# Tile 2's queries and keys in the slots of late weights, tile 3's unit loads one by one

## The chip, the cores and the metric

The kernel runs on one core of a Trainium2 chip. The metric is the device time of one execution in microseconds (us); lower is better. Five engines work side by side, each through its own queue in order: TensorE (PE; its weight loads are PEld), VectorE (DVE), ScalarE (ACT), GpSimd (POOL) and SyncE (SP), which here issues most of the DMA transfers.

## The reference, cut to what matters

Sliding-window attention (4 batches, 8 heads, 576 positions, 64 features, each query sees itself and the 63 positions ahead of it), then two feed-forward layers over the 2304 tokens.

```python
def _attn_ref(q, k, v):
    scores = scale * np.matmul(q, k.transpose(0, 1, 3, 2))
    scores = np.where(mask, scores, -1e9)              # window of 64
    attn = exp(scores - max); attn = attn / (sum + 1e-9)
    return np.matmul(attn, v)

def _moe_ref(x, w_in, w_out):                          # 512 -> 2048 -> 512
    h = x @ w_in
    g = np.where(h >= 1, h, np.where(h <= -1, 0.0, (h + 1) ** 2 / 4))
    return g @ w_out

def _moe2_ref(x, w_in, w_out, g_ln):                   # 512 -> 1024 -> 512
    h = x @ w_in
    solu = h * softmax(h)
    return ((solu - mean) / sqrt(var + 1e-6) * g_ln) @ w_out
```

## The kernel before

Products of 32-bit numbers are made of three products each: every operand is split into a high part (`xh`, `gh`, `wih`, `woh`) and the remainder (`xl`, `gl`, `wil`, `wol`).

The first part of the program does attention and the first feed-forward layer at once. Tokens go in blocks of 384 (`j`), each of two tiles of 192 tokens (`t`); a tile has four groups of two heads (`g = 4 t + hp`). The 2048 features go in 16 ranges of 128 (`f`). For each block and range TensorE makes h (`ps_h`, `moe_h`), ScalarE and VectorE make the activation (`u` by `moe_g2` on VectorE, which is the last to read `ps_h` and so frees its bank; `gh` on ScalarE; `gl`, in block 0 on GpSimd), and TensorE adds it, times w_out, to four sums (`acc`, `moe_y`). `ps_h` has two banks, so a range waits for `u` of the range two before it. In block 0 ranges 0 and 1 go in two halves of 192 tokens. Between the ranges a slot of the attention of the next block is done (`slots`): scores (`ps_s`, `st_s`; VectorE's score reads make `p` and `mx`), probabilities, `ps_x`, and of that `xh` and `xl`.

Block 0 also brings in the weights. They come in 32 units, w_in and w_out of a range in turn (`w1_unit`, loads on SP of 512 KB into the staging tiles `wst`, of which there are five). A unit is prescaled on ScalarE (`split_a`), passed over twice on VectorE (`split_b`, L136 and L137), copied on ScalarE into `wih` or `woh`, and subtracted on VectorE (`split_c`, L146) into `wil` or `wol`. That last pass frees the staging tile for the unit five later. The result stays in SBUF, one slot for each range.

Queries and keys come in two ways (`load_qk`). Groups 0 to 11 (tiles 0 to 2) come a whole tile at a time as rows (`qkn`) and are transposed by TensorE (`st_qkt`, `ps_t`). From group 12 (tile 3) on they come as units, one for each group: eight loads of 24 or 32 KB in pieces of 32 numbers, which VectorE transposes in blocks of 32 x 32 (L331, L332). The rows of tiles 0 and 1 lie in slots of w_in ranges 12 to 15, not yet used; the rows of tile 2 take four of the five tiles `qk`, in which the units lie too. The four units of tile 3 are asked for together, at group 11 (`qkt_and_loads`).

A scheduler sets the order of each engine's queue from its own estimate of times; the code gives dependencies and buffers, and `tc.issue_after(x)` asks that what is traced in it stand behind instruction `x` on the engine of `x`. `wdma` lists the weight loads.

## Time and profile before

| | us |
|---|---|
| median of 3 runs | 706.5 (705.88 to 707.57) |
| the profiled execution | 706.22 |
| its span, first to last instruction | 704.1 |
| TensorE busy in the span | 682.2 |
| VectorE busy | 441.7 |
| ScalarE busy | 412.3 |
| GpSimd busy | 153.8 |

The 2.1 us between the profiled execution's time and its span lie around the first and the last instruction. Busy times are averages over stages with different limits; the rows further down go by stretches of time.

### The profile page before, as it was taken

Reading aid. Unit: us, or ns where it says so; the run is one execution under the profiler, and the core shown is the slowest. Engines: PE = TensorE matmul, PEld = TensorE weight load, DVE = VectorE, ACT = ScalarE, POOL = GpSimd, SP = SyncE. Lnnn points to the kernel's source line nnn. Section 1 sums busy time; section 2 is a strip of 40 time slices with the busy share of each in tenths; the row PEclk is TensorE's granted clock in tenths of the full one; section 3 lists DMA queues with packets and bytes.
Section 4 is the critical chain, followed back from the end, with each engine's and each line's share of the span. In section 5 each row is a group of like instructions: output and inputs, shape, how many; then the busy total and the mean of one; then the engine's idle time right before and its main releaser. Section 6 shows DMA issues by size and latency. Waiting matters only on the chain.

```text
span 704.1 us, 12633 instructions
## 1 busy us (share of the span) xinstructions
PE 682.2 (97%) x4439; PEld 629.4 (89%) x4439; DVE 441.7 (63%) x1179; ACT 412.3 (59%) x1006; POOL 153.8 (22%) x193
## 2 busy tenths in 40 slices
PE   6969999999999999999999999999999999999998
PEld 5858899999999999999999999999987788888887
DVE  4699888356455555454455553642379999988850
ACT  5898877465556655565566565354454746345451
POOL 3432422200001000021112111652272322220000
PEclk9988999999999999999999999999999999999999
DMA  9997486534354524345352211562024465534321
GB/s 188 225 260 227 125 243 152 115 75 108 72 115 107 120 64 78 74 129 130 79 113 70 99 49 42 173 202 90 1 100 124 151 194 168 185 126 142 128 90 46
DMA packets 150391, 87.62 MB, mean 124 GB/s; under 512 B 113464, under 2 KB 136248, under 8 KB 150328
## 3 DMA queue, kind: packets, MB, share of 16 engines
q1 hardware_dynamic: 138888, 62.69, 35.9%
q0 software_dynamic: 8704, 19.41, 8.4%
q10 hardware_dynamic: 2736, 4.72, 1.8%
q8 instruction: 35, 0.57, 0.4%
q14 instruction: 28, 0.23, 0.1%
HBM read 62.66 MB, written 24.12 MB: 123 GB/s over the span
## 4 chain that ended last, share of the span: by engine, by line
PE 78%; DVE 7%; issue 5%; ACT 4%; DMA 2%; POOL 2%; SPq 1%; DVEq 0%; POOLq 0%; ACTq 0%
PE acc L533 25%; PE ps_h L502 24%; PE ps_o L832 13%; PE P L717 8%; PE ps_x L482 2%; PE ps_s L448 2%; PE ps_p L408 2%; POOL wil L249 2%; PE ps_s L358 1%; PE ps_x L427 1%; DVE gl L522 1%; DVE wst L137 1%; DMA wst<-in_moe_w_in_dram 1%; ACT p L372 1%; DMA wst<-in_moe_w_out_dram 1%
## 5 line engine op out<-in xcount | busy, mean ns | idle before, releaser
L517 DVE SCALAR_TENSOR_TENSOR u<-u,ps_h 128x384 f32<-128x384 f32 (+1 forms) x98 | 53.3, 544 | 144.1 <-ACT u L512 143.5
L502 PE MATMUL ps_h<-xh,wih 128*128 128x384 f32 (+1 forms) x392 | 132.4, 339 | 4.6 <-DVE u L517 3.6
L502 PE MATMUL ps_h<-xl,wih 128*128 128x384 f32 (+1 forms) x392 | 132.3, 338 | 1.7 <-DVE xl L435 1.7
L533 PE MATMUL acc<-gl,woh 128*128 128x384 f32 (+1 forms) x392 | 130.7, 334 | 1.6 <-DVE gl L522 1.3
L502 PE MATMUL ps_h<-xh,wil 128*128 128x384 f32 (+1 forms) x392 | 131.9, 337 | 0.0
L533 PE MATMUL acc<-gh,wol 128*128 128x384 f32 (+1 forms) x392 | 129.6, 332 | 0.0
L533 PE MATMUL acc<-gh,woh 128*128 128x384 f32 (+1 forms) x392 | 128.9, 341 | 0.4 <-ACT gh L518 0.4
L511 ACT ACTIVATE u<-ps_h,half 128x384 f32<-128x384 f32 (+1 forms) x98 | 56.1, 573 | 92.3 <-PE ps_h L502 92.1
L518 ACT CAST gh<-u 128x384 fp32r<-128x384 f32 (+1 forms) x98 | 49.7, 507 | 56.1 <-DVE u L517 38.7
L502 PEld LDWEIGHTS ps_h<-xh,wih 128*128 128x128 f32 x392 | 74.5, 191 | 5.9 <-DVE u L517 4.0
L502 PEld LDWEIGHTS ps_h<-xl,wih 128*128 128x128 f32 x392 | 74.7, 191 | 2.7 <-DVE xl L435 2.1
L533 PEld LDWEIGHTS acc<-gl,woh 128*128 128x128 f32 x392 | 73.7, 188 | 2.5 <-DVE gl L522 1.7
L533 PEld LDWEIGHTS acc<-gh,woh 128*128 128x128 f32 x392 | 72.7, 188 | 3.6 <-issue 2.6
L502 PEld LDWEIGHTS ps_h<-xh,wil 128*128 128x128 f32 x392 | 74.8, 191 | 0.2 <-DVE wil L146 0.2
L522 DVE TENSOR_TENSOR gl<-u,gh 128x384 fp32r<-128x384 f32 x80 | 51.0, 638 | 37.4 <-ACT gh L518 36.8
L533 PEld LDWEIGHTS acc<-gh,wol 128*128 128x128 f32 x392 | 73.6, 188 | 0.0
L717 PE MATMUL P<-wih,x2p 128*128 128x512 f32 x216 | 70.8, 391 | 1.4 <-DVE xo L545 0.9
L832 PE MATMUL ps_o<-woh,wol 128*128 128x512 f32 (+1 forms) x152 | 57.7, 380 | 0.3 <-DVE wol L820 0.3
L832 PE MATMUL ps_o<-woh,woh 128*128 128x512 f32 (+1 forms) x152 | 57.7, 379 | 0.0
L832 PE MATMUL ps_o<-wol,woh 128*128 128x512 f32 (+1 forms) x152 | 57.5, 378 | 0.0
L512 ACT ACTIVATE u<-u 128x384 f32<-128x384 f32 (+1 forms) x98 | 51.1, 521 | 2.0
L717 PEld LDWEIGHTS P<-wih,x2p 128*128 128x128 f32 x216 | 40.5, 188 | 10.4 <-DVE xo L545 1.3
(126 smaller groups left out, 1217.0 us busy)
## 6 DMA issues: line engine op xcount, KB each, us to landing
wst<-in_moe_w_in_dram SPq DMA_DIRECT2D x16, 512.0 KB, 5.5
wst<-in_moe_w_out_dram SPq DMA_DIRECT2D x16, 512.0 KB, 5.3
lnd<-e SPq DMA_DIRECT2D x16, 512.0 KB, 2.8
lT<-lnd SPq DMA_DIRECT2D x64, 128.0 KB, 3.0
vw<-in_v_dram SPq DMA_DIRECT2D x24, 256.0 KB, 4.9
x2d<-xo POOLq DMA_DIRECT2D x24, 192.0 KB, 2.4
out_dram<-o ACTq DMA_DIRECT2D x17, 256.0 KB, 2.4
wst<-in_moe_w_in_dram POOLq DMA_DIRECT2D x8, 512.0 KB, 5.5
```

What stands on the lines that cost most here:

```text
L249: nc.gpsimd.tensor_tensor(lo, v_, as_f32(hi), op=ALU.subtract)
L408: nc.tensor.transpose(ps[:, i * 128:i * 128 + 128], p[:, i, :], ident)
L448: nc.tensor.matmul(ps[x][64 * c:64 * c + 64, i * 128 + c0:i * 128 + 128], z[r, KQ + i * 64:KQ + i * 64 + 64], z[r, i * 64 + c0:i * 64 + 12 ...
L502: nc.tensor.matmul(ps, a, bb[:, kc, c], start=(n == 0), stop=(n == 3 * KC - 1))
L511: nc.scalar.activation(u, ps, ACTF.Relu, bias=half, scale=0.5)
L512: nc.scalar.activation(u, u, ACTF.Square)
L517: g = nc.vector.scalar_tensor_tensor(u, u, 1.0, ps, op0=ALU.min, op1=ALU.max)
L518: return nc.scalar.copy(hi, u).ins, g.ins
L522: eng.tensor_tensor(lo, u, as_f32(hi), op=ALU.subtract)
L533: nc.tensor.matmul(acc[j, e][:, c], a, bb, start=(f == 0 and n == 0 and c.start == 0), stop=(f == NF - 1 and n == 2),)
L717: nc.tensor.matmul(ps, l, r, start=(n == 0), stop=(n == 5))
L832: nc.tensor.matmul(ps, a[kk // 4][:, kk % 4, :], b[kk][:, c:c + w], start=(n == 0), stop=(n == 3 * NK2 - 1),)
```

## The change

The rows of tile 2 no longer lie in tiles `qk`: its queries go to the slots `woh14` and `woh15`, its keys to `wol14` and `wol15`, the slots of w_out of the last two ranges. The tiles `qk` are then free for units from the start. The units of tile 3 are asked for one at each of the groups 8 to 11 instead of all at group 11, and each stands behind the weight load issued last (`wdma[-1]`) instead of behind the first one (`wdma[0]`).

```diff
                 for r in range(2):
-                    if t < 2:
-                        a = w_p.tile([128, 512], F32, tag=f"{tag}{14 - 2 * t + r}", name="qkn")
-                    else:
-                        a = at_p.tile([128, 512], F32, tag="qk", bufs=5, name="qkn")
+                    if t == 2:
+                        tag = "woh" if src is q else "wol"
+                    a = w_p.tile([128, 512], F32, tag=f"{tag}{14 - 2 * (t % 2) + r}", name="qkn")
                     dst[t, r] = a[0:n, :]
...
         if m >= NPE and m + 4 < NG:
             load_qk(m + 4)
-        if m == NPE - 1:
-            for z in range(1, 5):
-                after(load_qk, m + z)
+        if NPE - 4 <= m < NPE:
+            with tc.issue_after(wdma[-1]):
+                load_qk(m + 4)
```

The scheduler makes other queues of it. Lines behind the change count one less than before. On VectorE, about the second half of ranges 0 and 1, `wst_626` before and `wst_635` in the change are unit 11, `wil5` is the third pass of unit 10, and `u_729`, `u_812` before are `u_747`, `u_830` in the change. Before, from `xl` on:

```order
L435 TENSOR_TENSOR xl_312<-ps_x_664,xh_311 128x192
L383 TENSOR_SCALAR sm_654<-sm_654 128x3
L136 TENSOR_SCALAR wst_626<-wst_626 128x512
L137 SCALAR_TENSOR_TENSOR wst_534<-wst_534 128x512
L384 RECIPROCAL rs_673<-sm_654 128x3
L137 SCALAR_TENSOR_TENSOR wst_626<-wst_626 128x512
L146 TENSOR_TENSOR wol4_524<-wst_525,woh4_523 128x512
L146 TENSOR_TENSOR wil5_533<-wst_534,wih5_532 128x512
L517 SCALAR_TENSOR_TENSOR u_729<-u_729,ps_h_716 128x192
L146 TENSOR_TENSOR wol5_625<-wst_626,woh5_624 128x512
L517 SCALAR_TENSOR_TENSOR u_812<-u_812,ps_h_799 128x192
```

The same place in the change, from `xl` on as well:

```order
L434 TENSOR_TENSOR xl_312<-ps_x_673,xh_311 128x192
L137 SCALAR_TENSOR_TENSOR wst_525<-wst_525 128x512
L146 TENSOR_TENSOR wil4_500<-wst_501,wih4_499 128x512
L136 TENSOR_SCALAR wst_534<-wst_534 128x512
L342 COPY kq1_125<-ps_t_693 64x3x64
L382 TENSOR_SCALAR sm_663<-sm_663 128x3
L137 SCALAR_TENSOR_TENSOR wst_534<-wst_534 128x512
L146 TENSOR_TENSOR wol4_524<-wst_525,woh4_523 128x512
L383 RECIPROCAL rs_682<-sm_663 128x3
L516 SCALAR_TENSOR_TENSOR u_747<-u_747,ps_h_734 128x192
L136 TENSOR_SCALAR wst_635<-wst_635 128x512
L516 SCALAR_TENSOR_TENSOR u_830<-u_830,ps_h_817 128x192
```

`xl` moved ahead of four rows that stood before it (`wil4`, the copy to `kq1` and two passes), and unit 11's passes and the third of unit 10 moved behind the first `u`; unit 11's first pass stands ahead of the second `u`.

On SP, the loads from unit 10 (`wst_534`) on. Before, weights follow each other with three loads of v between them, and the units of tile 3 come later:

```order
L124 DMA wst_534<-in_moe_w_in_dram 128x4x256
L126 DMA wst_626<-in_moe_w_out_dram 128x1024
L307 DMA vw_692<-in_v_dram 128x8x64
L304 DMA vw_694<-in_v_dram 64x8x64
L307 DMA vw_1297<-in_v_dram 128x8x64
L124 DMA wst_630<-in_moe_w_in_dram 128x4x256
L126 DMA wst_710<-in_moe_w_out_dram 128x1024
L124 DMA wst_714<-in_moe_w_in_dram 128x4x256
```

In the change, with the units of groups 12 (`qk_613`) and 13 (`qk_701`); `wst_635` is unit 11, `wst_728` unit 13:

```order
L124 DMA wst_534<-in_moe_w_in_dram 128x4x256
L290 DMA qk_613<-in_q_dram 32x6x32 x4
L290 DMA qk_613<-in_k_dram 32x6x32 x4
L126 DMA wst_635<-in_moe_w_out_dram 128x1024
L124 DMA wst_639<-in_moe_w_in_dram 128x4x256
L290 DMA qk_701<-in_q_dram 32x6x32 x4
L290 DMA qk_701<-in_k_dram 32x6x32 x4
L306 DMA vw_710<-in_v_dram 128x8x64
L303 DMA vw_712<-in_v_dram 64x8x64
L126 DMA wst_728<-in_moe_w_out_dram 128x1024
L124 DMA wst_732<-in_moe_w_in_dram 128x4x256
```

Eight loads of a unit now stand between units 10 and 11, and eight more between units 12 and 13. Two further groups of eight stand behind units 16 and 20, and the eight loads of group 12, which stood ahead of and among units 5 and 6, are gone from there.

On VectorE, between `u` of range 6 (`u_1201` in both) and `u` of range 7 (`u_1279` in both). Before, behind the score reads, which follow `u_1201`:

```order
L331 STREAM_TRANSPOSE kq1_125<-qk_977 64x3x64 x2
L332 STREAM_TRANSPOSE kq1_125<-qk_977 128x192
L383 TENSOR_SCALAR sm_1064<-sm_1064 128x3
L384 RECIPROCAL rs_1102<-sm_1064 128x3
L517 SCALAR_TENSOR_TENSOR u_1279<-u_1279,ps_h_1266 128x384
L435 TENSOR_TENSOR xl_772<-ps_x_1093,xh_771 128x192
```

In the change, behind the transposes; `wst_1113`, `wst_1117` and `wst_1182` are units 23 to 25, and the first pass of `wst_1113` stands right behind `u_1201`:

```order
L146 TENSOR_TENSOR wol10_1035<-wst_1036,woh10_1034 128x512
L137 SCALAR_TENSOR_TENSOR wst_1113<-wst_1113 128x512
L146 TENSOR_TENSOR wil11_1039<-wst_1040,wih11_1038 128x512
L136 TENSOR_SCALAR wst_1117<-wst_1117 128x512
L136 TENSOR_SCALAR wst_1182<-wst_1182 128x512
L382 TENSOR_SCALAR sm_1064<-sm_1064 128x3
L137 SCALAR_TENSOR_TENSOR wst_1117<-wst_1117 128x512
L434 TENSOR_TENSOR xl_790<-ps_x_1093,xh_789 128x192
L137 SCALAR_TENSOR_TENSOR wst_1182<-wst_1182 128x512
L383 RECIPROCAL rs_1102<-sm_1064 128x3
L146 TENSOR_TENSOR wol11_1112<-wst_1113,woh11_1111 128x512
L516 SCALAR_TENSOR_TENSOR u_1279<-u_1279,ps_h_1266 128x384
```

Nine passes of weight units moved to this place, where none stood.

## Rows read from the trace of the kernel before

**Rows 1.** Busy time by engine in stretches of time, with the granted clock.

```profile
core 0: us, PE busy (x) PEld busy (x) DVE busy (x) ACT busy (x) POOL busy (x), PEclk, DMA share, GB/s
36.65:53.13 16.48, 10.18 (x91) 8.89 (x90) 16.17 (x44) 14.85 (x41) 5.15 (x6) 0.83 1.02 264
53.13:74.85 21.72, 20.78 (x141) 19.76 (x142) 20.66 (x53) 18.02 (x40) 4.91 (x5) 0.89 0.77 245
...
85.00:704.00 619.00, 612.40 (x3959) 567.36 (x3958) 374.17 (x972) 344.22 (x809) 125.93 (x150) 1.00 0.41 113
```

**Rows 2.** Waits of TensorE, whole span: total us, times, longest.

```profile
PE ps_h L502 <- DVE u L517: 3.6, 2, 3.0
...
PE acc L533 <- ACT gh L518: 0.4, 1, 0.4
```

**Rows 3.** Timeline of TensorE: start, us, instruction, idle time before it.

```profile
53.53 0.69 PE L502 MATMUL ps_h<-xh,wih 128*128 128x384 f32 x1 [3.02 <-DVE u L517]
54.02 0.52 PE L502 MATMUL ps_h<-xl,wih 128*128 128x384 f32 x1
...
70.38 0.44 PE L502 MATMUL ps_h<-xh,wih 128*128 128x384 f32 x1 [0.54 <-DVE u L517]
```

**Rows 4.** Timeline of VectorE, 48.94 to 54.34 us and 86 to 90.5 us.

```profile
48.94 0.34 DVE L435 TENSOR_TENSOR xl<-ps_x,xh 128x192 fp32r<-128x192 f32 x1
...
51.90 1.31 DVE L146 TENSOR_TENSOR wil<-wst,wih 128x512 fp32r<-128x512 f32 x1
53.13 0.34 DVE L517 SCALAR_TENSOR_TENSOR u<-u,ps_h 128x192 f32<-128x192 f32 x1
...
54.00 0.34 DVE L517 SCALAR_TENSOR_TENSOR u<-u,ps_h 128x192 f32<-128x192 f32 x1
...
86.03 0.55 DVE L517 SCALAR_TENSOR_TENSOR u<-u,ps_h 128x384 f32<-128x384 f32 x1 [0.71 <-ACT u L512]
...
90.10 0.43 DVE L136 TENSOR_SCALAR wst<-wst 128x512 uint32<-128x512 uint32 x1 [3.25 <-DMA wst<-in_moe_w_in_dram]
```

**Rows 5.** Chain that ended last, near 92 us: start, us, merged instructions.

```profile
92.36 2.08 PE ps_h L502 x12
```

**Rows 6.** VectorE's instructions by group, 53.13 to 86.5 us: busy us, mean ns.

```profile
L137 DVE SCALAR_TENSOR_TENSOR wst<-wst 128x512 uint32<-128x512 uint32 x12 | 8.9, 752 | 0.6 <-ACT wst L132 0.5
L146 DVE TENSOR_TENSOR wil<-wst,wih 128x512 fp32r<-128x512 f32 x7 | 5.4, 773 | 0.4 <-ACT wih L145 0.4
L136 DVE TENSOR_SCALAR wst<-wst 128x512 uint32<-128x512 uint32 x12 | 5.2, 434 | 0.5 <-DMA wst<-in_moe_w_out_dram 0.5
L146 DVE TENSOR_TENSOR wol<-wst,woh 128x512 fp32r<-128x512 f32 x7 | 5.0, 720 | 0.0
...
L366 DVE CUSTOM_DVE_ANT_0 p<-ps_s,mask 128x128 f32<-128x128 f32 x9 | 2.1, 283 | 0.0
L331 DVE STREAM_TRANSPOSE kq<-qk 64x192 f32<-64x192 f32 x4 | 1.5, 370 | 0.0
```

**Rows 7.** Waits of SP's queue, 90 to 102 us: total us, times, longest.

```profile
SPq L291 <- DMA wst<-in_moe_w_in_dram: 2.4, 3, 1.6
```

**Rows 8.** Timeline of SP: when it issued some loads, and how long that took.

```profile
42.81 0.37 SPq L124 DMA_DIRECT2D wst<-in_moe_w_in_dram  x1
...
73.67 1.79 SPq L291 DMA_DIRECT2D qk<-in_q_dram  x4
...
86.07 0.39 SPq L124 DMA_DIRECT2D wst<-in_moe_w_in_dram  x1
86.56 1.90 SPq L291 DMA_DIRECT2D qk<-in_q_dram  x4
...
92.04 0.39 SPq L124 DMA_DIRECT2D wst<-in_moe_w_in_dram  x1
```

**Rows 9.** The load issued at 42.81 us: time from issue to landing.

```profile
DMA to landing us min/median/max: 4.4/4.4/4.4
```

**Rows 10.** The w_in loads issued at 86.07, 91.01 and 92.04 us: issue to landing.

```profile
DMA to landing us min/median/max: 4.0/5.1/7.3
```

## The prediction

> **What bounds the kernel now.** First the stretches. From 85 us to the end TensorE is busy 612.4 of 619 us: whatever moves its work at 85 us moves the end by as much [rows 1]. Before that it is not the bound. Between 36.65 and 53.13 us it is busy 10.18 of 16.48 us while VectorE is busy 16.17, and in the next 21.72 us VectorE has 1.06 us free [rows 1]. The waits of TensorE name the place: the products of x with w_in waited 3.6 us for `u` on VectorE, which frees their PSUM bank [rows 2]. The timeline shows 3.02 us of it ahead of 53.53 us, where range 2 begins, and 0.54 us at 70.38 us, where range 5 begins [rows 3]. At 53.53 us the clock is at the lower of its two levels (0.52 us for a product of 384 columns) [rows 3]. VectorE's timeline says why `u` came late: passes of weight units stood ahead of it in the queue, the last from 51.90 to 53.13 us [rows 4]. Later the sign turns: at 86.03 us `u` of range 7 waits for ScalarE, and until 90.10 us VectorE stands idle 3.25 us for a weight load [rows 4]. TensorE does not notice: its chain runs through, range 9 begins at 92.36 us [rows 5].
>
> So the time before 85 us is a race of VectorE's queue against TensorE. I number weight units from 0, w_in and w_out of a range in turn: unit 10 is `wih5`/`wil5`, unit 11 `woh5`/`wol5`, unit 13 `woh6`/`wol6`, unit 27 `woh13`/`wol13`. VectorE passes over each three times: first, second, third pass (L136, L137, L146).
>
> **The slots.** Queries and keys of tile 2 now lie in the slots of w_out ranges 14 and 15. In the changed order the third pass into `wol14` stands some 60 rows of VectorE behind the copy of the last transposes that read them. Price 0; with that cover gone it would cost a pass or two.
>
> **Less queued ahead of `u` (ranges 0 and 1, second half).** The first pair of order rows shows it: both early passes of unit 11 and the third of unit 10 no longer stand ahead of the first `u`. That is 0.35 + 0.67 us (mean durations less the 0.08 us by which an instruction overlaps the next) [rows 6] and 1.23 us (51.90 to 53.13) [rows 4], 2.25 us. `xl` stands four places further ahead, so TensorE and ScalarE do not hold `u` instead. Range 2 begins at 53.5 - 2.25 = 51.3 us. Bounds: 50.0, if the earlier `xl` spares waits upstream too, and 52.5, if ScalarE takes half back.
>
> **A new wait: the first pass of unit 11 ahead of the second `u`.** Each load of SP's queue signals one of eight semaphores in turn, so the ninth waits for the landing of the one eight before it. The trace shows that after 90 us, where unit loads waited three times, 2.4 us in all, for w_in loads [rows 7]. The change puts eight unit loads between units 10 and 11 (second pair of order rows), so that the eighth waits for unit 10. Unit 10 is issued at 42.81 us [rows 8] and lands 4.4 us later [rows 9], at 47.2; a unit load takes SP some 0.45 us (1.79 us for four) [rows 8]. So unit 11 goes out at 47.8 and lands at 52.2, unit 12 at 52.9. The second `u` follows at 52.6 us, still ahead of its old 54.00 [rows 4]. TensorE wants that bank only after the twelve products of range 2, which take 2.1 us at the full clock [rows 5] and twice that at the lower level: at 53.4 to 55.5 us. Hidden, price 0; with unit 10 taking 7.3 us [rows 10] `u` would come at 55.5, and the cover would be used up.
>
> **The second group of eight** ends by waiting for unit 12 (52.9). Two loads of v follow, so unit 13 goes out at 54.4 us and units 14 to 16 at steps of 0.45. For landings I take 4.2 us for the first and 7.3 for the fourth: the last of four weight loads issued together (at 92.04 us) took 7.3, the one at 86.07 us 4.0 [rows 8, 10]. Unit 13 is there at 58.6, unit 16 at 63.1. Bounds for unit 13: 57.5 (each step 0.4 us shorter) and 61.5 (each load of the chain 1.5 us longer).
> VectorE, by the same prices, is through with `u` of range 2 at 56.8 us and stands still until 58.6: the first pass of unit 13 is next, ahead of the score reads of the next group. Nobody waits yet, since TensorE has ranges 3 and 4 to do.
>
> **From there VectorE's queue decides.** In the order of the change there stand, from the first pass of unit 13 to `u` of range 7: 13 first passes of 0.35 us, 13 second of 0.67, 11 third (6 `wol` of 0.64, 5 `wil` of 0.69), 5 `u` of 0.47, 9 score reads of 0.20, 6 transposes of 0.37 and 11 small ones of some 0.24 (`xl` takes 0.26 [rows 4], the others less or as much): 4.6 + 8.7 + 7.3 + 2.4 + 1.8 + 2.2 + 2.6 = 29.6 us [rows 6]. The third group of eight ends by waiting for unit 16 (63.1), so unit 17 goes out at 63.6 and lands at 67.8, where VectorE has stood since about 66.0: 1.8 us. The fourth ends by waiting for unit 20; unit 21 lands near 78.0, when VectorE gets there: 0. `u` of range 7 ends at 58.6 + 29.6 + 1.8 = 90.0 us, where it ended at 86.6 (86.03 and 0.55) [rows 4]. The third pair of order rows shows why: three first (one ahead of the score reads), three second and three third passes now stand between `u` of range 6 and of range 7, and none did.
> Range 9 needs that bank. It began at 92.36 us bound by TensorE alone [rows 5]; now it begins at 90.1, 2.3 us earlier. The head start would allow 2.25 us at range 2, the 0.54 at 70.38 [rows 3] and the 0.4 us of the wait for `gh` [rows 2], 3.2 together; VectorE gives back 0.9.
> On ScalarE `gh` of range 7 now stands behind the prescale of unit 27, which goes out near 87.4 us behind two unit loads and lands near 91.8; TensorE asks for `gh` at 90.1 + 2.1 = 92.2. I take 0.5 us, between 0 (it lands first) and 2.9 (7.3 us for 4.4). Left: 1.8 us. Behind range 9 both kernels have the last weights in VectorE's queue, and `u` of range 9 falls near 101 us, when TensorE asks for it: 0, at most 1.
>
> **The sum.** The profiled execution took 706.2 us (704.1 us of span and 2.1 around it); less 1.8 that is 704.4. The median of the runs is 0.3 us above it, so 704.4 to 704.7: I say 704.5.
>
> **Rivals.**
> Carried through: 3.2 us reach the end, or 4.2 with the waits upstream. It needs unit 13 by 57.5 us and landings of 4.0 us throughout; `u` of range 7 then ends at 88.2. For it: single loads took 4.0 and 4.4 us [rows 9], and unit loads are spread out. Against it: four weight loads still go out together. 702 to 703.2 us.
> Given back whole: `u` of range 7 ends at 91.5 to 92.5 us and TensorE begins range 9 as before: 705.5 to 706.8. One more stall of 1.5 us in the chain of landings does it.
> Slower: the chain of landings itself. Units 10, 12, 16 and 20 are each waited for by the last load of a group, and each microsecond by which one lands later moves units 13, 17 and 21. From 92.3 us on each microsecond of `u` of range 7 is one of the end. With 1.5 us more at each of the first three it ends at 94 us, and the time is 708. For it: loads in company took up to 7.3 us [rows 10].
> The Trainium skill ("DMA: Bandwidth & Descriptors", section Specifications) speaks for this rival: transfers of under 512 B a piece stay below line rate, as the engine reads and modifies before it writes. The unit loads move pieces of 128 B, and by that rule weight loads among them would be held up and the time be this rival's. The trace bears it out little: the load at 86.07 us lay between groups of unit loads and took 4.0 us, the least of its stretch [rows 8, 10].
>
> **How the numbers follow.** Chances: the forecast (1 to 3 us gained) 0.42, carried through 0.18, given back 0.21, slower 0.19. Less than 0.2% (1.4 us) cannot be told from no change here. Of the forecast 0.32 lie above 1.4 us, with the carried 0.18 faster is 0.50; the rest of it and the given-back case make 0.31; slower 0.19. The range goes from 702.0 (carried through, waits upstream spared) to 708.0 (the slower rival at 1.5 us a load), with about 0.1 left out on either side. The forecast's own range is 703.2 to 705.2.
>
> **What would show it.** Range 2 should begin at 50 to 52.5 us. SP should issue unit 11 near 47.8, unit 13 near 54.4 and unit 17 near 63.6 us, each behind a unit load that waited for a weight. VectorE should stand idle for weight loads near 51, 57 to 59 and 66 to 68 us, and next to nothing from 86 to 90. `u` of range 7 should end near 90 us, and range 9 begin right behind it. I am wrong if VectorE stands still for more than 4 us near 58, if TensorE waits for `u` in ranges 4 to 7 already, or if a difference arises in the last two thirds of the program, where both orders agree.

## The result

The change made the kernel slower: 710.2 us (708.99 to 711.15, six runs) against 705.9 us (705.37 to 707.57, six runs); both figures are medians, and the ratio of the means is 1.0055 (95% interval 1.004 to 1.007). I had forecast 704.5 us, in a range of 702.0 to 708.0. The run that was profiled took 708.99 us, with a span of 707.2 us, 3.1 us more than before.

### The profile page after: what moved, and what is told of

It reads as the page before. It is cut to its first block, busy times and chain, and to the rows that moved or that the text cites. A ratio compares the mean times of both kernels' runs of the same rounds, so it can differ in the third digit from the quotient of the medians.

```text
span 707.2 us, 12615 instructions
## 1 busy us (share of the span) xinstructions
PE 681.0 (96%) x4439; PEld 627.9 (89%) x4439; DVE 443.1 (63%) x1179; ACT 412.5 (58%) x1006; POOL 154.7 (22%) x193
## 4 chain that ended last, share of the span: by engine, by line
PE 76%; DVE 7%; issue 5%; DMA 4%; ACT 3%; POOL 2%; SPq 1%; POOLq 0%; DVEq 0%; ACTq 0%
PE acc L532 23%; PE ps_h L501 23%; PE ps_o L831 13%; PE P L716 8%; DMA wst<-in_moe_w_in_dram 2%; PE ps_x L481 2%; DMA wst<-in_moe_w_out_dram 2%; POOL wil L249 2%; PE ps_p L407 2%; PE ps_s L447 2%; ACT p L371 1%; PE ps_s L357 1%; DVE gl L521 1%; DVE wst L137 1%; PE ps_x L426 1%
## 5 line engine op out<-in xcount | busy, mean ns | idle before, releaser
L521 DVE TENSOR_TENSOR gl<-u,gh 128x384 fp32r<-128x384 f32 x80 | 52.4, 655 | 37.4 <-ACT gh L517 36.8
L511 ACT ACTIVATE u<-u 128x384 f32<-128x384 f32 (+1 forms) x98 | 51.3, 523 | 2.0
```

What stands on the lines that cost most here:

```text
L511: nc.scalar.activation(u, u, ACTF.Square)
L521: eng.tensor_tensor(lo, u, as_f32(hi), op=ALU.subtract)
```

## The profile after, read against the rows of before

Busy time by engine in the stretches of [rows 1], with the granted clock (PEclk):

```profile
36.65:53.13 16.48, 11.50 (x82) 10.66 (x81) 16.18 (x37) 14.23 (x39) 6.04 (x7) 0.86 0.64 181
53.13:74.85 21.72, 20.87 (x148) 19.78 (x148) 17.64 (x46) 17.07 (x42) 5.54 (x5) 0.95 0.84 238
...
85.00:704.00 619.00, 610.64 (x3933) 565.05 (x3931) 378.09 (x978) 346.60 (x818) 127.08 (x151) 1.00 0.41 111
```

In the first stretch TensorE is busy 1.3 us longer than before, since range 2 falls into it. In the second VectorE is busy 17.64 us where it was busy 20.66: it stands still for weights (3.3 us of waits in that stretch, in [rows 6] 0.5). From 85 us on TensorE, which was the bound there, is no longer busy throughout: 8.4 us are free of 619, where 6.6 were.

Waits of TensorE over the whole span (total us, times, longest), to be held against [rows 2]:

```profile
PE ps_p L407 <- POOL p L391: 4.0, 4, 2.5
...
PE ps_h L501 <- DVE u L516: 2.7, 1, 2.7
...
PE ps_p L407 <- DVE p L391: 1.4, 1, 1.4
```

The wait for `u` shrank from 3.6 to 2.7 us, but another heads the list, and a second one stands further down, that the prediction does not name: the transposes `ps_p` wait for the probabilities `p` of the attention, 2.5 us at one place and 1.4 at another. TensorE's timeline has both (start, us, instruction, idle time before it):

```profile
49.23 0.69 PE L501 MATMUL ps_h<-xh,wih 128*128 128x384 f32 x1 [2.70 <-DVE u L516]
...
88.84 0.34 PE L532 MATMUL acc<-gh,wol 128*128 128x384 f32 x1
91.70 0.55 PE L407 MATMUL ps_p<-ident,p 128*128 128x128 f32 x3 [2.52 <-POOL p L391]
92.08 0.83 PE L357 MATMUL ps_s<-kq 128*128 128x64 f32 x6
92.67 0.53 PE L501 MATMUL ps_h<-xh,wih 128*128 128x384 f32 x1
...
96.19 0.37 PE L501 MATMUL ps_h<-xh,wil 128*128 128x384 f32 x1
96.40 0.86 PE L532 MATMUL acc<-gh,woh 128*128 128x384 f32 x4
...
137.06 0.52 PE L407 MATMUL ps_p<-ident,p 128*128 128x128 f32 x3 [1.37 <-DVE p L391]
```

Range 2 begins at 49.23 us, 4.3 us earlier than in [rows 3], and range 9 at 92.67 us. Before, TensorE's timeline has its first product at 92.20 us, so it is 0.5 later (the row of [rows 5], 92.36, is the chain's and begins a little behind it):

```profile
92.20 0.33 PE L502 MATMUL ps_h<-xh,wih 128*128 128x384 f32 x1
```

Behind the pause the twelve products of range 9 run at the lower of the two clock levels (0.53 us each; granted clock 0.54) and take 3.7 us instead of 2.08:

```profile
92.67:96.40 3.73, 3.73 (x15) 3.73 (x14) 2.52 (x5) 2.37 (x6) 1.31 (x1) 0.54 1.02 245
```

That the clock falls there is not the rule: the run change_again, which is the change once more, has a pause of 2.50 us at this place and a granted clock of 0.50 from 93.25 to 95.09 us; the run change_late, with the same order up to there, has one of 2.53 us and runs on at the upper level. VectorE's timeline says why `p` was late:

```profile
87.40 0.68 DVE L146 TENSOR_TENSOR wil<-wst,wih 128x512 fp32r<-128x512 f32 x1
88.00 0.75 DVE L136 TENSOR_SCALAR wst<-wst 128x512 uint32<-128x512 uint32 x2
88.67 0.15 DVE L382 TENSOR_SCALAR sm<-sm 128x3 f32<-128x3 f32 x1
88.74 0.68 DVE L137 SCALAR_TENSOR_TENSOR wst<-wst 128x512 uint32<-128x512 uint32 x1
89.35 0.34 DVE L434 TENSOR_TENSOR xl<-ps_x,xh 128x192 fp32r<-128x192 f32 x1
89.62 0.67 DVE L137 SCALAR_TENSOR_TENSOR wst<-wst 128x512 uint32<-128x512 uint32 x1
90.22 0.15 DVE L383 RECIPROCAL rs<-sm 128x3 f32<-128x3 f32 x1
...
90.88 0.54 DVE L516 SCALAR_TENSOR_TENSOR u<-u,ps_h 128x384 f32<-128x384 f32 x1
```

The sum `sm` is ready at 88.8 us, but the reciprocal `rs` comes only at 90.22, behind the second passes of units 24 and 25; GpSimd multiplies `p` after it, and TensorE's queue has the transposes of that `p` ahead of range 9. `u` of range 7 ends at 91.4 us, so range 9 could not have begun before that even if `p` had come early.

SP's timeline and its waits between 36 and 90 us show the line of loads:

```profile
54.91 2.66 SPq L290 DMA_DIRECT2D qk<-in_q_dram  x4
57.63 5.56 SPq L290 DMA_DIRECT2D qk<-in_k_dram  x4
63.29 0.39 SPq L126 DMA_DIRECT2D wst<-in_moe_w_out_dram  x1
```

```profile
SPq L290 <- DMA wst<-in_moe_w_in_dram: 7.6, 6, 2.3
SPq L290 <- DMA wst<-in_moe_w_out_dram: 2.6, 4, 1.1
```

Unit loads waited 10.2 us for weights to land, 4.2 of it in the third group of eight (54.91 to 63.19 us); unit 17 went out behind it, at 63.29 us.

Where the 3.1 us arise is seen from when the same range begins, on TensorE's timeline of both:

| first product of | before | after | after is later by |
|---|---|---|---|
| range 8 | 87.00 | 83.86 | -3.1 |
| range 10 | 97.08 | 99.19 | 2.1 |
| range 15 | 123.60 | 123.74 | 0.1 |
| range 9 of block 1 | 175.17 | 177.72 | 2.55 |
| end of the span | 704.1 | 707.2 | 3.1 |

In this profile three microseconds are won up to range 8 and 5.2 lost between ranges 8 and 10: 3.2 us are waits for `gl` (0.70) and `p` (2.52), 1.65 the lower clock.

The lead of 3.1 us, however, is that of one execution. Five of the runs below have the order of the change on TensorE and VectorE up to range 8, and before_late has that of before (us; idle is VectorE's waiting for weights to land, 48 to 86 us):

| kernel | range 2 begins | range 8 begins | idle |
|---|---|---|---|
| before | 53.53 | 87.00 | 0.5 |
| before_late | 53.27 | 86.05 | 0 |
| change | 49.23 | 83.86 | 4.7 |
| change_again | 49.45 | 85.55 | 7.1 |
| rs_first | 51.24 | 87.59 | 6.6 |
| u7_first | 49.16 | 85.93 | 8.2 |
| change_late | 51.26 | 85.81 | 5.3 |
| u7_late | 50.83 | 86.21 | 6.8 |

The lead at range 2 (2 to 4 us) is there in all six. At range 8 the other five are between 1.5 us ahead of before and 0.6 behind it: most of the lead is gone before range 9, while VectorE stands still for weights. The loss between ranges 8 and 10 comes on top in all of them (table of the experiments). Up to range 15 the change seems to catch up, but it has done one group of attention less by then: before, TensorE makes the transposes and scores of a group in range 10, after it makes none between 99.19 and 107.56 us. The group (1.7 us: 0.35 for `ps_p` and 0.74 for `ps_s` from 137.06 us on, 0.61 for `ps_x`) is made up between block 0 and block 1, where nothing covers its chain of waits: the 1.37 us above. Behind that the two kernels run alike to 0.5 us, which arise in the last 207 us with TensorE equally busy and are not explained.

## The experiments

The theories: **queue** (VectorE's order in range 7 makes the loss), **line** (unit loads between weight loads on SP make weights late, and VectorE's order only follows; the expectations speak of landing, issue or SP theory as well), **small pieces** (pieces of 128 B slow the weight loads that travel with them), **boundary** (the attention that is late at the end of block 0). Each ratio is to the kernel before on the same chip. The last two columns are read from TensorE's timeline of one profiled execution, so that the different starts drop out: from the first product of range 8 to that of range 10, and from range 15 to range 9 of block 1. Two profiles of the change itself agree to 0.3 us in them, although one began range 8 1.7 us later. The edits alter the scheduler's orders too; where that matters it is said. The kernels do not all do the same attention in these stretches: by the instructions for `ps_p`, four_long and four_late transpose no group from 8 to 10, where the others transpose one, and from 15 to block 1's 9 before, before_late and passes_behind_u transpose seven groups, pool_queue six and the others eight. long_pieces, four_long and four_late read other numbers into tile 3, so their attention there is not the reference's; they serve for their times alone.

| kernel | ratio (95%) | 8 to 10 | 15 to block 1's 9 |
|---|---|---|---|
| before | 1 | 10.1 | 51.6 |
| change (first profile; change_again) | 1.0055 (1.0038 to 1.0071) | 15.3; 15.0 | 54.0; 54.0 |
| rs_first | 1.0067 (1.0046 to 1.0088) | 14.6 | 54.0 |
| u7_first | 1.0054 (1.0037 to 1.0071) | 13.4 | 54.1 |
| passes_behind_u | 1.0070 (1.0049 to 1.0091) | 10.9 | 54.7 |
| slots_alone | 1.0046 (1.0031 to 1.0061) | 12.2 | 54.1 |
| long_pieces | 1.0079 (1.0058 to 1.0099) | 14.1 | 54.8 |
| four_long | 0.9990 (0.9972 to 1.0008) | 10.7 | 54.0 |
| pool_queue | 1.0150 (1.0122 to 1.0177) | 11.1 | 49.1 |
| half_units | 1.0118 (1.0095 to 1.0141) | 11.0 | 59.6 |
| sixteen | 1.0085 (1.0059 to 1.0111) | 11.5 | 53.4 |
| rows_tile3 | 1.0065 (1.0038 to 1.0092) | 13.2 | 58.9 |
| change_late | 1.0043 (1.0025 to 1.0062) | 14.5 | 52.5 |
| half_late | 1.0033 (1.0017 to 1.0049) | 11.2 | 54.3 |
| rows_late | 1.0014 (0.9999 to 1.0030) | 13.0 | 54.4 |
| before_late | 0.9990 (0.9974 to 1.0006) | 10.1 | 50.6 |
| four_late | 0.9975 (0.9962 to 0.9988) | 10.6 | 52.4 |
| u7_late | 1.0014 (0.9999 to 1.0029) | 14.5 | 52.5 |
| rows_u24 | 0.9979 (0.9962 to 0.9995) | 11.7 | 53.6 |

### VectorE's order in range 7

**rs_first** and **u7_first**: for units 24 and 25,

```diff
-            split_b(*w_b[-1])
+            with tc.issue_after(x):   # x: rs of group 11; in u7_first u of range 7
+                split_b(*w_b[-1])
```

> The change, with the first and second passes over units 24 and 25 put behind the reciprocal `rs` of group 11 on VectorE; nothing else. Queue theory (the loss is made on VectorE in range 7: `rs` of group 11 and `u` of range 7 stand behind those passes, TensorE stands still 2.5 us ahead of the transposes `ps_p` and then runs the twelve products of range 9 at the lower clock, 3.7 us instead of 2.1): `rs` comes at about 88.1 instead of 90.2 us, `ps_p` at about 89.7 instead of 91.7, but `u` of range 7 keeps its end near 91.3, so range 9 begins at 91.4 instead of 92.7: 1.3 us gained, 708.9, and up to 1.8 more if the shorter pause leaves the clock up. Landing theory (weights that land late make the loss, 4.3 us of idle VectorE ahead of units 13, 17 and 21, and whatever is won at one place is lost at the next): 710. Boundary theory (the loss is the group of attention that left range 10 and is made up between block 0 and block 1): the wait of 1.4 us at 137 us stays, and the time with it.

> The change, with the first and second passes over units 24 and 25 put behind `u` of range 7 on VectorE, and so behind `rs` of group 11 as well. Queue theory: `u` of range 7 ends near 89.6 instead of 91.4 us, `ps_p` stands no longer than 0.7 us, range 9 begins near 90.1 instead of 92.7 us: 2.6 us gained, 707.6, with the clock staying up 1.8 more, 705.8. Landing theory: the four passes (2 us) then hold the next `u`s, and ranges 10 to 13 begin where they began: 709.5 to 710.2. Boundary theory: the pause near 137 us stays, so no less than 707.

Neither was faster than the change, by intervals that leave room for some 1 us. TensorE's timeline of rs_first has the transposes of `p` and range 9, and that of u7_first the sums before and behind them too:

```profile
93.37 0.55 PE L415 MATMUL ps_p<-ident,p 128*128 128x128 f32 x3 [0.23 <-POOL p L399]
...
96.19 0.44 PE L509 MATMUL ps_h<-xh,wih 128*128 128x384 f32 x1 [1.33 <-DVE u L524]
```

```profile
89.12 0.44 PE L540 MATMUL acc<-gl,woh 128*128 128x384 f32 x1 [0.78 <-POOL gl L529]
91.54 0.55 PE L414 MATMUL ps_p<-ident,p 128*128 128x128 f32 x3 [0.23 <-POOL p L398]
92.56 0.44 PE L508 MATMUL ps_h<-xh,wih 128*128 128x384 f32 x1
...
96.62 0.44 PE L540 MATMUL acc<-gl,woh 128*128 128x384 f32 x1 [1.09 <-POOL gl L529]
```

The long wait for `p` is gone in both (0.23 us), and the products of range 9 run at the upper level (granted clock 1.00 from 96.19 and from 92.56 us on). That the wait had its cause in those passes is shown. In rs_first TensorE then waits 1.33 us for `u` of range 7, the next in line. In u7_first the gain from range 8 to 10 is 1.6 to 1.9 us, but a wait of 1.09 us for `gl` follows in the next sums, the late group is made up at the boundary as before, and the forecast of 705.8 to 707.6 us is missed (710.6). The queue theory alone falls.

**passes_behind_u** does the same for every unit from 18 on.

> The change, with the first and second passes over every unit from 18 on put behind the `u` that the program makes just ahead of them. Queue theory: no `u` and no `rs` from range 5 on waits behind passes that are not wanted yet; TensorE keeps its lead of 3 us at 86 us through range 9, and only the pause between the blocks (1.4 us) remains: 704 to 706. Landing theory: the passes are late for the products that need their weights, and TensorE waits for `wih` and `wil` from range 10 on: 709 to 713. Boundary theory: the group of attention is made up between the blocks as in the change: 707 at least.

It is the same story in larger: 10.9 us from range 8 to 10, but 30.1 from range 10 to 15 where the change took 24.6 to 25.8 (with a group of attention less), and 1.0070 in all. The time is what the landing theory forecast; TensorE waited for `pT`, `u` and `xl` there, though (4.7 us with `p`), and not for `wih` or `wil`.

**slots_alone** keeps the new slots and the old loads.

```diff
-        if NPE - 4 <= m < NPE:
-            with tc.issue_after(wdma[-1]):
-                load_qk(m + 4)
+        if m == NPE - 1:
+            for z in range(1, 5):
+                after(load_qk, m + z)
```

> Only the slots of the change: tile 2's rows in `woh14`, `woh15`, `wol14`, `wol15`, and tile 3's units asked for together at group 11 as before. The tiles are free from the start, so the scheduler brings all four units in ahead of unit 10 (39 unit loads among units 4 to 11), and none among units 11 to 17. Landing theory: units 11 to 22 come without unit loads between them, VectorE does not stand still for units 13, 17 and 21, and the time is 704 to 706. Queue theory: in the order `rs` of group 11 stands behind two second and three first passes again (units 20 to 22) and `u` of range 7 behind one more, so TensorE stands still in range 7 to 9 for 1 to 3 us as in the change: 708 to 711. Boundary theory: here too TensorE does no attention in range 10 and makes up a group between the blocks: 1 to 2 us above before, 707 to 708.

1.0046 (710.2 us): within the change's interval, and in the queue theory's range (708 to 711), not in the landing theory's (704 to 706). With the tiles free, the scheduler brings the unit loads in even earlier, and range 2 began at 55.4 us. So the new slots cost as much with the old way of asking. What the second half of the change, which holds the loads back, does by itself is not shown, and the run does not part weights from order either: VectorE stood still 11.1 us for weights between 48 and 95 us, where the landing theory expected it not to.

### SP's line and the small pieces

**change_again** is the control.

> The change once more, without an edit, beside the next three on the same chip. All theories: 1.0055 times the kernel before (1.004 to 1.007). Landing theory besides: where the first profile had VectorE idle 4.3 us for units 13, 17 and 21, this one has 3 to 6 us, as landings differ from run to run, and TensorE's waits between 53 and 90 us differ with them.

It came out as said. Its TensorE waited for `p` at the same place:

```profile
93.25 0.90 PE L407 MATMUL ps_p<-ident,p 128*128 128x128 f32 x3 [2.50 <-POOL p L391]
```

**long_pieces** reads tile 3's units in pieces of 768 or 1024 B, **four_long** also in half as many loads. The edit of four_long (long_pieces has only a pattern of its own for `s_`, and eight loads):

```diff
+                if t == NPE // NP:
+                    s_ = src[b, 2 * hp + x, r0:r0 + n, :].rearrange("(j m) d -> j (m d)", j=64)
+                    nc.sync.dma_start(out=a[64 * x:64 * x + 64, m0:m0 + n // 32, :], in_=s_.rearrange("j (m i) -> j m i", i=32))
+                    continue
```

> The change, with the unit loads of tile 3 (groups 12 to 15) read in whole pieces of 768 or 1024 B instead of 128 B, eight loads of the same bytes per unit as before; these groups then hold other numbers, so their attention is not the reference's. Small-pieces theory (the pieces of 128 B hold up the weight loads that travel with them): weight loads land in 4 to 5 us instead of 4 to 8.6, units 13, 17 and 21 come 1 to 2 us earlier each, and the time is 706 to 707.5. SP theory (what counts is that eight issues of 0.49 us stand between two weight loads, and that one of them waits for a weight load to land): units 13 and 17 move by at most 1 us, 709 to 710.5. Boundary theory: the order still makes up one group of attention between the blocks, so no less than 707.

> As the kernel with whole pieces, and each unit of tile 3 in four loads of 64 partitions instead of eight of 32; the same numbers are wrong. SP theory: 2 us less of issuing a group, and the signal that a unit load waits for is that of an older load, so units 13 and 17 go out 2 to 4 us earlier (by 50 and 58 us), VectorE stands idle for them less than 1.5 us in all, and the time is 705 to 707. Small-pieces theory: the same time as with eight whole-piece loads, within 0.7. Boundary theory: no less than 707.

Times from issue to landing of units 13 to 16, the group of four that went out together, in the change and in long_pieces:

```profile
DMA to landing us min/median/max: 4.9/6.6/8.6
```

```profile
DMA to landing us min/median/max: 5.1/6.8/8.1
```

The long pieces changed nothing in these landings, and the time did not fall. The small-pieces theory falls, and with it, as a cause here, the rule of the Trainium skill ("DMA: Bandwidth & Descriptors", section Specifications) that transfers under 512 B stay below line rate: no cost of the pieces of 128 B beside the weights can be measured in this kernel. four_long was 4.2 us faster than the change (707.1 against 711.3 in the same group of runs, the intervals lie apart). Its unit loads' waits for landings between 36 and 90 us:

```profile
SPq L294 <- DMA wst<-in_moe_w_in_dram: 0.9, 1, 0.9
...
SPq L294 <- DMA wst<-in_moe_w_out_dram: 0.6, 1, 0.6
```

They are 1.5 us instead of 10.2 (weight loads wait 0.7 more), unit 17 went out at 58.5 us instead of 63.3, and VectorE waited 1.4 us for weights between 48 and 90 us, where it waited 4.7 in the change. That this is the number of loads alone is not shown: in four_long's order the transposes of group 11, for which range 9 stood still in the change, come only after range 10 has begun. Up to range 15 both kernels have transposed as many groups; from range 8 to there four_long takes 37.3 us, the change 39.9 and 40.9.

**pool_queue** issues tile 3's unit loads from GpSimd.

```diff
-                    nc.sync.dma_start(out=a[p0:p0 + 32, m0:m0 + n // 32, :], in_=s_[e])
+                    eng.dma_start(...)   # eng: nc.gpsimd for tile 3
...
-            with tc.issue_after(wdma[-1]):
+            with tc.issue_after(pp[-1]):   # the multiplication of p made last
```

> The change, with tile 3's unit loads on GpSimd's queue, each group behind the probabilities of the group that the program made last there; SP issues only weights and v between units 10 and 26, and the output is the reference's. SP theory: units 11 to 17 go out as staging tiles come free, none behind a unit load, VectorE is not idle for units 13 and 17, and the time is 703 to 705.5, if `gl` on GpSimd is not held by the eight issues of some 0.55 us in front of it (up to 4.4 us a group; where it is, TensorE waits for `gl` and 706 to 708 come out). Small-pieces theory: the pieces travel beside the weights as before, weights still land in 5 to 8 us, 707 to 710. Boundary theory: the order makes up no group between the blocks here, so 1 to 3 us are won by that alone: 707 to 709 with the rest unchanged.

1.015: the reason is in part the one named in the expectation, only larger. GpSimd's timeline:

```profile
57.72 0.57 POOL L292 DMA_DIRECT2D qk<-in_q_dram  x1 [1.06 <-issue]
60.65 0.56 POOL L292 DMA_DIRECT2D qk<-in_k_dram  x1 [2.36 <-issue]
61.49 1.75 POOL L292 DMA_DIRECT2D qk<-in_k_dram  x3 [0.28 <-issue]
63.25 1.15 POOL L523 TENSOR_TENSOR gl<-u,gh 128x192 fp32r<-128x192 f32 x2
```

The issues stall GpSimd's queue, and `gl` stands behind them: TensorE waits 3.0 us for it between 50 and 100 us. The longest wait there, 3.50 us ahead of range 8 at 100.3 us, is for `u` on VectorE, and what made that late is not traced. It says nothing against the line theory, and nothing for it. Its boundary stretch is the shortest of all (49.1 us), since its order makes up no group there.

**half_units** keeps the eight loads and the small pieces, but asks for the four of q and the four of k behind different weights; **sixteen** halves each load.

```diff
             with tc.issue_after(wdma[-1]):
-                load_qk(m + 4)
+                load_qk(m + 4, (0,))        # q; k follows behind the next w_load(2)
```

```diff
+                        for c in range(0, n // 32, 4):   # sixteen
+                            nc.sync.dma_start(out=a[p0:p0 + 32, m0 + c:m0 + d, :], in_=s_[e][:, c:d])
```

> The change, with each unit of tile 3 asked for in two parts: the four loads of q behind the weight load issued last, the four of k behind the next pair of weight loads. As many loads of the same 128 B pieces as in the change, all of tile 3's in the same stretch, but four in a row instead of eight. Landing theory (what costs is that the eighth load of a group waits for the landing of the weight ahead of the group, 10 to 12 us of SP's queue between 36 and 90 us): a load of the second four waits for a weight issued two weights before, which has landed; SP's waits for landings fall below 4 us, VectorE stands idle for weights below 2 us, and the time is 705.5 to 707.5. Issue theory (it is the 0.49 us that SP takes for each of the 32 loads, 16 us in all): as many issues, so units 13, 17 and 21 come no more than 1 us earlier, 709 to 711. Boundary theory: the order makes up a group and a half between the blocks, so no less than 707.

> The change, with each unit of tile 3 in sixteen loads of half the size: the same bytes and pieces, twice the loads. Issue and landing theories together (SP's line between weights): 4 us more of issuing a group and one more round of waits for landings; units 13, 17 and 21 go out 4, 10 and 15 us later than in the change, VectorE's idle time for them doubles or more, and the time is 714 to 720. Boundary theory, and any theory in which the order of the attention alone counts: within 1.5 of the change, 709 to 712.

Both missed their times. In half_units the stretch from range 8 to 10 fell from 15 to 11.0 us with the same attention in it, yet the kernel was the slowest but one: the stretch at the boundary rose from 54.0 to 59.6. Nor did the line get as short as the edit was to make it: unit loads still waited 7.2 us for landings (below 4 expected) and VectorE 3.5 us for weights (below 2), so the 11.0 us are not shown to be the line's. TensorE's timeline there, and the stretch behind it by windows:

```profile
137.93 0.86 PE L410 MATMUL ps_p<-ident,p 128*128 128x128 f32 x3 [3.41 <-DVE p L394]
...
140.88 0.69 PE L504 MATMUL ps_h<-xh,wih 128*128 128x384 f32 x1 [0.81 <-DVE mx L368]
```

```profile
141.00:145.00 4.00, 4.00 (x14) 3.64 (x15) 1.29 (x4) 0.70 (x4) 0.00 (x0) 0.53 0.60 135
```

Its order, too, has the transposes and scores of a group between the blocks; TensorE waits 3.41 us for `p`, then 0.81 for the score reads, and runs on at the lower clock (granted clock 0.53).

In sixteen the weights came as late as expected (unit 17 at 75.4 us, unit 21 at 89.9), and VectorE stood still for them:

```profile
66.67 0.43 DVE L136 TENSOR_SCALAR wst<-wst 128x512 uint32<-128x512 uint32 x1 [4.73 <-DMA wst<-in_moe_w_out_dram]
79.37 0.43 DVE L136 TENSOR_SCALAR wst<-wst 128x512 uint32<-128x512 uint32 x1 [3.11 <-DMA wst<-in_moe_w_out_dram]
...
94.06 0.43 DVE L136 TENSOR_SCALAR wst<-wst 128x512 uint32<-128x512 uint32 x1 [2.19 <-DMA wst<-in_moe_w_out_dram]
```

But by the ratios it was only 2 us slower than the change, not 4 to 10, and the intervals overlap. Weights that go out 12 to 15 us later do not cost 12 us: TensorE waits for none of them between 86 and 128 us. Why they cost so little is not shown; that less stood behind their passes in VectorE's queue is a guess.

**rows_tile3** brings tile 3 as rows too, four loads instead of 32.

```diff
-    NPE = 3 * NP
+    NPE = 4 * NP
...
+        if m == NPE - 8:
+            with tc.issue_after(wdma[-1]):
+                load_qk(NPE - 4)
```

> The change carried on to tile 3: its queries and keys come as rows in four loads too (slots `woh14`, `woh15`, `wol14`, `wol15`; tile 2's move to `woh12`, `woh13`, `wol12`, `wol13`), asked for at group 8, and TensorE transposes them; unit loads start with group 16. The output is the reference's. Line theory (issue or landing): 4 loads instead of 32 between units 10 and 24, so VectorE never waits for units 13, 17 or 21; VectorE saves the block transposes of four groups (some 1.1 us each) and copies a quarter of them instead, TensorE gets 4 x 4 transposes more (some 0.5 us a group): 703 to 706. Boundary theory: a group and a half is made up between the blocks, 707 to 709.

With no unit load between the weights range 8 began at 80.3 us, 3.6 us ahead of the change and 6.7 of before. Of the 6.7 us 2.4 were left at range 15 (121.2 us), and the boundary took 7.3 (58.9 us against 51.6). This, with half_units, made the boundary a theory to be tested by itself.

### The boundary

The **late** kernels move two steps of attention behind the start of block 1 and leave the order up to there as it was.

```diff
-            slot(n1)
+            slot(n1 + ((1 if j == 1 and f in (2, 3) else 0) - (1 if j == 0 and f in (14, 15) else 0)))
```

> The change, with one attention step fewer in each of ranges 14 and 15 of block 0 and one more in each of ranges 2 and 3 of block 1: the transposes of group 16 and the scores of group 17 then stand behind the first twelve products of block 1 on TensorE; up to there the order is that of the change. Boundary theory: the wait of 1.4 us at 137 us goes, and nothing else: 1 to 1.5 us faster than the change, 1.0035 to 1.004 of the kernel before. If the boundary made the whole loss: 1.000. Landing theory alone: no difference to the change, 1.005 to 1.0055.

> Tile 3's units in two parts as in the run half_units, and the two attention steps moved behind the start of block 1. Both causes theory: the waits of 85 to 115 us are 1.9 us as there, the 6.9 us at the boundary (4.2 idle, the rest lower clock) shrink to 1.5 to 3 since the chain of group 15 still has to end there: 4 to 5 us faster than half_units, 1.005 to 1.006 of the kernel before, and 1.000 if the clock does not fall at all. Landing theory alone: as half_units, 1.010 to 1.012.

> Tile 3 as rows as in the run rows_tile3, and the two attention steps moved behind the start of block 1. Both causes theory: of 5.6 us at the boundary 2 to 4 go: 1.001 to 1.004 of the kernel before. Landing theory alone: as rows_tile3, 1.005 to 1.008.

> The kernel before, with the two attention steps moved in the same way. It has no wait at the boundary but 0.3 us ahead of the products with the values, so no theory expects a gain: 0.999 to 1.001 of the kernel before; by as much as it is off, the move itself costs or wins something.

In the change the wait at 137 us went and the stretch fell by 1.5 us; the ratio went from 1.0055 to 1.0043, which the intervals don't tell from nothing. In half_units, where the boundary cost most, the same edit won 6 us (1.0118 to 1.0033, intervals apart), in rows_tile3 3.6 us. The kernel before, which has no wait there, stayed as it was. The boundary is shown as a cause of its own in half_units and rows_tile3, where it eats what was won earlier. In the change as it stands it is 1.5 us of a stretch and can't be told from nothing in the time.

### Both together

**four_late** is four_long with the two steps moved, **u7_late** is u7_first with them, **rows_u24** is rows_late with the passes of units 24 to 31 behind the `u` made ahead of them.

> Tile 3's units in four whole-piece loads as in the run four_long (these groups hold other numbers), and the two attention steps moved behind the start of block 1. Line and boundary as the two causes: four_long stood at 0.999 with a wait of 1.4 us left at the boundary, so 0.996 to 0.998 of the kernel before, 1 to 2 us faster than it. If the boundary costs nothing once the line is short: 0.999 to 1.000.

> The change with the passes over units 24 and 25 behind `u` of range 7 (as u7_first) and the two attention steps moved (as change_late); SP's queue stays as in the change. Line theory: VectorE's order is a consequence, so what is won at range 9 is lost by range 12 again, and only the boundary's 1 us is won: 1.004 to 1.0055 of the kernel before. Queue theory: both waits go, 1.000 to 1.002.

> Tile 3 as rows and the two attention steps moved (as rows_late), and the first and second passes over units 24 to 31 put behind the `u` that the program makes just ahead of them. If `u` is held by passes at the head of VectorE's queue whose weight has not landed (1.9 and 0.9 us in the run rows_late): up to 2 us faster than rows_late, 0.998 to 1.000 of the kernel before. If the weights are then late for their own products: 1.002 to 1.005.

four_late came out as expected: 705.6 us, 0.9975 of before. u7_late leaves SP's line alone and still stands at 1.0014, 3 us better than the change, where u7_first and change_late taken singly had no gain that can be measured. That was the queue theory's forecast for the two waits together, and not the line theory's. Its one profile, of an execution of 710.0 us where the median is 708.8, does not show where the gain is.

rows_u24 is the version with the reference's output that beats both before and the change: 706.1 against 707.1 us of before, 0.9979 (0.9962 to 0.9995). VectorE's timeline of rows_late shows what held `u`, and that of rows_u24 that it no longer does:

```profile
92.70 0.43 DVE L136 TENSOR_SCALAR wst<-wst 128x512 uint32<-128x512 uint32 x1 [1.88 <-DMA wst<-in_moe_w_out_dram]
93.04 0.69 DVE L137 SCALAR_TENSOR_TENSOR wst<-wst 128x512 uint32<-128x512 uint32 x1
93.64 0.55 DVE L516 SCALAR_TENSOR_TENSOR u<-u,ps_h 128x384 f32<-128x384 f32 x1
```

```profile
91.48 0.55 DVE L523 SCALAR_TENSOR_TENSOR u<-u,ps_h 128x384 f32<-128x384 f32 x1 [2.26 <-ACT u L518]
91.96 0.76 DVE L136 TENSOR_SCALAR wst<-wst 128x512 uint32<-128x512 uint32 x2
```

In the first a pass waits 1.88 us at the head of the queue for a weight that has not landed, and `u` stands behind it; in the second `u` goes first and waits for ScalarE only. SP's queue is the same in both.

## Why the prediction was wrong, point by point

**Slots: price 0.** Right: no wait of the profile is put down to them. But free tiles let the scheduler write other orders, which the price left out: slots_alone costs as much as the whole change.

**Less queued ahead of `u`.** Right: range 2 began at 49.2 to 51.3 us in six profiles of this order, where 51.3 was forecast. 49.2 is below the lower bound of 50.0.

**The wait of unit 11, hidden.** Right: the second `u` came at 50.1 us and nobody waited for it.

**The groups of eight.** The mechanism was right: units 13 and 17 went out at 52.6 and 63.3 us (54.4 and 63.6 forecast), each behind a unit load that waited. The sizes were too small. In the first profile VectorE stood still 1.62 and 1.47 us where I had 1.8 and 1.8, and 1.19 at unit 21, where I had 0; in all it waited 4.7 us for weights, and 5.3 to 8.2 in the five other profiles of this order, for 3.6 in the sum. The fourth load of four landed after 8.6 to 9.4 us in the six instead of 7.3, and unit 13 after 4.7 to 6.2 instead of 4.2.

**"`u` of range 7 ends at 90.0 us".** This term was mis-sized: 91.4 in the first profile, where the stall of 1.19 us is most of it, and 93.0 and 93.4 in change_again and change_late, whose VectorE order is the same up to there.

**"Range 9 needs that bank ... now it begins at 90.1".** This step failed. `u` is not all that range 9 waits for: TensorE's queue has the transposes of group 11 ahead of it, and their `p` waits for `rs` on VectorE. The third pair of order rows, which the prediction used only to count passes ahead of `u`, shows `rs_1102` behind two second passes in the change. Range 9 began 2.6 us later than forecast: by 1.4 us `u` itself was late, and the other 1.2 are the transposes and scores that had stood still behind `p`. Its products took 1.65 us more at the lower clock. For these last two the sum had no term. By range 10 the forecast (97.1 less 2.3, plus 0.5) was 95.3 us, and it was 99.2: 3.9 of the 4.9 us by which the profiled span was missed.

**"Behind range 9 ... 0, at most 1".** The size is at its bound, the other 1.0 us, but the step had no mechanism for it: the order drops a group of attention in range 10 and makes it up at the boundary, where 1.37 us of waiting come with it, and 0.5 us arise near the end of the program. I had said that the orders agree in the last two thirds; there the profiles run alike to these 0.5 us.

**The rivals.** The slower one named the line of landings and came nearest (708). It wanted 1.5 us more at units 10, 12 and 16. Unit 10 landed as forecast (3.9 to 4.3 us in the six profiles), unit 12 after 5.2 to 6.1, for about 4.6 in the sum, and unit 16 after 8.6 to 9.4 for 7.3: in good part it happened. Yet landings are not the whole: with the line in place, moving two things out of its way left 1.0014, and with half the loads the loss was gone, though in another order.

**What stays open.** How much of the loss is the line's and how much VectorE's order that follows from it can't be separated further: every edit to the loads makes the scheduler write new orders on all engines, twice the loads cost far less than the line theory said, no run shortens the line with the orders kept, and where u7_late won its 3 us no profile shows.

## What to carry to other kernels

When an instruction is freed earlier, look at everything that stands ahead of it in the queue of the engine that is to profit, not only at the wait that was removed: here the next item in TensorE's queue hung on a reciprocal of 0.15 us that had moved behind weight passes. Count how much side work each kernel has done at the same landmark before calling a lead a lead; work that was skipped is paid later, at the place with the least cover. And read a lead from more than one execution: the 3 us of the first profile were 1.5 at most in five others. Whether small loads in front of large ones cost by their number is not settled here: half as many came with 4.2 us less, twice as many with 2 us more within the noise, and each with other orders.

## What the runs showed of the hardware that I had not expected

- Eight loads of 24 KB in a row on SP took 8.3 us (54.91 to 63.19) where the weight loads ahead of them had to land first, and four loads in a row without such a wait 1.95; with pieces of 768 or 1024 B instead of 128 the eight took 7.7, and the weights ahead of them landed as late.
- A load issued by GpSimd took 0.56 us there and could stand still 2.4 us ahead of its issue, with nothing in the profile that released it (the "issue" rows of pool_queue), while arithmetic waited behind it.
- Executions of the same kernel differ early: two profiles of the change began range 6 at 72.6 and 75.3 us with the same order of instructions, and VectorE waited 4.7 and 7.1 us for weights. A single profile told a stretch well, and the end time only to 2 or 3 us.
- The same pause of 2.5 us at the same place of the same order was followed by the lower clock in two profiles and by the upper one in a third (granted clock 0.54 and 0.50 against 1.00).
